# Turning one half of a token-mixing matrix before the attention inputs arrive, in an attention + mixer kernel

## The chip, the cores and the metric

The kernel runs on one core of one Trainium2 chip. The metric is device microseconds of one execution, as the median of the runs shown. A core has a matrix engine (TensorE: PE for its matmuls and PEld for its weight loads in the profile), three other compute engines (VectorE, DVE; ScalarE, ACT; GpSimd, POOL) and the sync engine (SP), each with its own in-order stream of instructions, and 16 DMA engines. Engines wait for each other through semaphores.

## The reference, cut to what matters

Attention over blocks that are mixed by a small doubly normalised matrix P comes first; its output, laid out as x with 768 tokens and 512 channels for each of 4 batches, goes through a residual mixer.

```python
P = sort_net                                   # [4, 8, 8, 8]
for _ in range(5):                             # "Sinkhorn": exp, then rows and columns normalised
    P = exp(P - max(P, -1)); P = P / sum(P, -1); P = P / sum(P, -2)
k_sorted = einsum('bhij,bhjcd->bhicd', P, k_b) # blocks of 96 keys, of 96 values, mixed by P
v_sorted = einsum('bhij,bhjcd->bhicd', P, v_b)
x = softmax(q_b @ k_sorted^T / 8) @ v_sorted   # inside each block of 96
...
a1  = alpha1 * x + beta1
tok = einsum('ts,bsd->btd', w_tok, a1)         # w_tok: 768 x 768, mixes tokens
u   = x + lam * tok
a2  = alpha2 * u + beta2
out = u + lam * (relu(a2 @ w_ch1) @ w_ch2)     # 512 -> 2048 -> 512
```

## The kernel before, in words

Batches 0 to 3 are worked through one after the other, each in two halves of 384 tokens. The channel mixer is the bulk: for every half, 16 groups of `h_ps` matmuls (`h_unit`) and 3 groups of `ch_ps` matmuls (`ch_unit`). The attention of batch b+1 is placed by hand between those groups (`put`, `run`, lines 861 to 949), so PE has channel work to do while the next batch's attention goes through the other engines. Batch 0 has no such cover: its attention is the start stage of the program, lines 794 to 852, and only its first half's channel work ends that stage.

Every engine's instructions are kept in the order in which the Python text issues them (`Engine`, lines 55 to 71). Tiles come from pools with a fixed number of buffers for each tag; a tile waits for the last use of the tile whose buffer it takes. PSUM has four small buffers (`psb`) and two of two banks (`psa`).

The start stage of batch 0, in order:

1. All large loads are DMAs that POOL issues: `q8` (two), `k8` (two), `v8` (two), the two halves of w_tok (`wt16`, two DMAs each), three broadcast vectors (`alphaB`, `betaB`, `lamB`), `W1p` and `W2p` (four each), then the raw values, keys and queries of batch 1 (`load_kv`, `load_q`). They cast from f32 to a 16-bit type. POOL's other work stands between them in the same stream.
2. The five Sinkhorn rounds (lines 302 to 319) alternate between ACT (the exponential) and DVE (sums, reciprocals, products). The table `beside` puts other work between rounds: turning the queries on PE (`q_first`), their copies out of PSUM (`q_out`), and `warm` matmuls on zeros, whose result nobody reads.
3. `mix_keys` and `mix_values` spread P into block matrices, `k_turn` and `k_copy` make the mixed, turned keys, `score` makes scores and exponentials (`et`, on ACT).
4. `v_sort` copies `v8` into `VD` with the feature index outermost, eight features a piece; `v_mix(0, n)` mixes the features 8n to 8n+7 on PE and copies them into `Vs[0]`. `pv_first(g)` needs all of `Vs[0]`; it multiplies by `et` and normalises into x on DVE, for two heads at a time.
5. The token mix of the first half of the tokens is done turned: `first_mm(g)` multiplies x by the first half of the turned w_tok (`w_tokT[:, :, 0:384]`), `first_turn(g)` turns x and adds the product of the row sums of w_tok (`rrow`) and lam·beta1 (`brow`). Out of both comes `a2T`, which the first `h_ps` matmul needs.

The turned w_tok is made in three steps for each half: `permute` copies `wt16` into `wp`, so that the 96 + 32 token rows of a panel lie side by side; `prep_wtok(ks, half)` turns panel ks in three PE transposes of 128 x 128 and copies it out of PSUM. The first half is done between the `pv_first` calls (lines 826 to 846), with row sums of w_tok by three ACT instructions (`row_sum`) that are turned in three more transposes. The second half's `prep_wtok` runs between the first `h_ps` groups.

Of the kernel before, what the change touches and what calls it, by code (L numbers as in the profile page):

```python
# [7 lines left out]
FT = mybir.dt.float32  # L8
# [8 lines left out]
def kernel(  # L17
# [25 lines left out]
    C = H * D  # L43
# [49 lines left out]
    def const(shape, dtype, name):  # L93
        return wts.tile(shape, dtype, name=name, tag=name)
# [22 lines left out]
    def load_slabs(dst, src):  # L117
        flat = src[0].rearrange("h s d -> (h s d)").rearrange("(g p f) -> p g f", p=128, f=12 * D)
        for g in range(0, H4, 2):
            pool.dma_start(dst[:, g:g + 2, :], flat[:, g:g + 2, :])  # L120

    def load_halves(dst, src):
        for th in range(2):
            pool.dma_start(
                dst[th * 64:(th + 1) * 64, :, :],
                src.rearrange("h (j th t) d -> th (h j) t d", j=NB, th=2)[th],
            )
# [12 lines left out]
    load_slabs(q8, q)  # L140
# [6 lines left out]
    dve.memset(brow[:].bitcast(FT), 0.0)  # L147
    dve.memset(rrow[:].bitcast(FT), 0.0)
# [3 lines left out]
    wt16 = []  # L152
    for half in range(2):
        t_ = att.tile([128, 3, S], F16, name="wt16", tag=("mixed", "qn")[half], bufs=1)
        for lo, n in ((0, 96), (TAIL, 32)):
            pool.dma_start(
                t_[lo // 6:lo // 6 + n],
                moe_w_tok[lo + 3 * half * n:lo + 3 * (half + 1) * n, :].rearrange("(tt p) s -> p tt s", p=n),
            )
        wt16.append(t_)  # L160
        if half == 0:
            pool.memset(VD[:, :, HB:64], 0.0)
            pool.memset(
                KT0[:].rearrange("p g i (th t) -> p (g i th) t", th=2)[:, :, HB:64].bitcast(FT), 0.0
            )

    def v_sort(lo, hi, eng):
        eng(VD[:, lo:hi, 0:HB], v8[:, :, lo:hi].rearrange("p t d -> p d t"))
# [7 lines left out]
    lamB = const([128, C], FT, "lamB")  # L176
    pool.dma_start(alphaB[:], moe_alpha1.partition_broadcast(128))
    pool.dma_start(betaB[:], moe_beta1.partition_broadcast(128))
    pool.dma_start(lamB[:], moe_lam.partition_broadcast(128))
    v_sort(16, 32, pool.tensor_copy)  # L180
    for g in range(4):
        if g == 1:
            v_sort(48, 64, pool.tensor_copy)
        pool.dma_start(W1p[:, :, g * 512:(g + 1) * 512], w1v[:, :, g * 512:(g + 1) * 512])
    pool.tensor_tensor(brow[0:1, :], bet1[:], lam1[:], ALU.mult)
# [12 lines left out]
    def load_kv(b):  # L198
        for kv, src in ((1, v), (0, k)):
            raw = att.tile([128, HB, D], F16, name="raw", tag="raw", bufs=2)  # L200
            load_halves(raw, src[b])
            raw_of[(b, kv)] = raw
# [26 lines left out]
    def warm(n, ps=psa):  # L229
        fill(ps([128, 512], FT, "warm_ps")[:], n)  # L230
# [29 lines left out]

    ab2col = const([128, 5 * CT], FT, "ab2col")

    def prep_ab2(ps):
        tps = ps([128, 4 * CT], FT, "ab2_ps")
        pe.transpose(tps[:], ab2[:], ident16f[:])
        act.copy(ab2col[:, 0:4 * CT], tps[:])
# [7 lines left out]
    rcol = const([128, 3], FT, "rcol")  # L274

    def row_sum(m):
        if m == 0:
            a1_of[0] = moep.tile([128, 8, C], F16, name="a1", tag="a1", bufs=1)
        act.activation(a1_of[0][:].rearrange("p k c -> p (k c)")[:, 0:S], wt16[0][:, m, :], AF.Copy, accum_out=rcol[:, m:m + 1])


# [5 lines left out]
    def q_first(g):  # L287
        qps[g] = q_turn(0, g, psa if g == 2 else psb)

    def q_out(g):  # L290
        for half in range(2):
            q_copy(0, g, qps[g], half, act.copy)

    beside = {
        0: [lambda: q_first(0), lambda: warm(3)],
        1: [lambda: q_first(1), lambda: warm(2), lambda: warm(3)],
        2: [lambda: q_first(2), lambda: warm(3)],
        3: [lambda: q_out(0), lambda: q_first(3)],
        4: [lambda: q_out(1), lambda: q_out(2), lambda: q_out(3), lambda: prep_ab2(psb), lambda: warm(4)],
# [20 lines left out]

    for g in range(4):
        pool.dma_start(W2p[:, g * 4:(g + 1) * 4, :], w2v[:, g * 4:(g + 1) * 4, :])
# [256 lines left out]
    w_tokT = const([128, NT, S], F16, "w_tokT")  # L579
    wp_of = {}  # L580

    def permute(half, eng, lo, hi):
        if lo == 0:
            wp_of[half] = (moep, att)[half].tile(
                [128, 3, NT, 128], F16, name="wp", tag=("u16", "raw")[half], bufs=(1, 2)[half]
            )
        wp = wp_of[half]
        src = wt16[half]
        for c0, n, w in ((0, 0, 96), (TAIL, 96, 32)):
            eng(  # L590
                wp[:, :, lo:hi, n:n + w],
                src[:, :, c0 + lo * w:c0 + hi * w].rearrange("p m (k c) -> p m k c", c=w),
            )

    def prep_wtok(ks, half, ps, eng):
        pst = ps([128, 384], F16, "wtok_ps")
        for m in range(3):
            pe.transpose(pst[:, m * 128:(m + 1) * 128], wp_of[half][:, m, ks, :], ident16[:])
        eng(w_tokT[:, ks, half * 384:(half + 1) * 384], pst[:])

    def row_sums(ps):
        rc16 = const([128, 3], F16, "rc16")
        act.copy(rc16[:], rcol[:])
        ps = ps([1, 384], F16, "rr_ps")
        for m in range(3):
            pe.transpose(ps[:, m * 128:(m + 1) * 128], rc16[:, m:m + 1], ident16[:])
        act.copy(rrow[0:1, :], ps[:])

# [17 lines left out]
    def moe_start(b):  # L626
        u_of[b] = []
        for hf in range(2):
            t_ = moep.tile([128, 3, C], FT, name=f"u32_{hf}", tag="u32", bufs=3)
            u_of[b] += [t_[:, kt, :] for kt in range(3)]  # L630
        a2T_of[b] = [moep.tile([128, CT, 384], BF, name=f"a2T_{hf}", tag="a2T", bufs=3) for hf in range(2)]
# [155 lines left out]
    def wtok(ks, eng):  # L787
        prep_wtok(ks, 0, psb, eng)

# [16 lines left out]
    v_sort(0, 8, act.copy)  # L806
    v_sort(8, 16, act.copy)
# [4 lines left out]
    v_sort(32, 48, copy)  # L812
    warm(2, psb)
    v_mix(0, 0, psb, copy)
    v_mix(0, 1, psb, copy)
    score(0, 1, 0, psa)
    v_mix(0, 2, psb, copy)
    v_mix(0, 3, psb, act.copy)
    score(0, 1, 1, psa)
    v_mix(0, 4, psb, copy)  # L820
    v_mix(0, 5, psb, copy)
    score(0, 2, 0, psa)
    v_mix(0, 6, psb, copy)
    v_mix(0, 7, psb, act.copy)
    score(0, 2, 1, psa)
    row_sum(0)
    permute(0, copy, 0, 3)
    moe_start(0)
    warm(1, psb)
    pv_first(0)  # L830
    score(0, 3, 0, psa)
    wtok(0, copy)
    wtok(1, act.copy)
    wtok(2, copy)
    permute(0, copy, 3, 6)
    row_sum(1)
    row_sum(2)
    pv_first(1)
    wtok(3, copy)
    wtok(4, copy)  # L840
    wtok(5, copy)
    permute(1, copy, 0, 6)
    score(0, 3, 1, psa)
    pv_first(2)
    row_sums(psb)
    first_mm(0, psb)
    first_turn(0, psb)
    first_mm(1, psb)
    pv_first(3)
    first_turn(1, psb)  # L850
# [3 lines left out]
    load_kv(1)  # L854
# [15 lines left out]
    for ks in range(NT):  # L870
        put(0, 0, "h", ks, lambda ks=ks: prep_wtok(ks, 1, psa, (dve.tensor_copy, act.copy)[ks % 2]))
# [108 lines left out]
```

## Time and profile before

| | |
|---|---|
| median of 3 runs | 264.29 us (263.53, 264.29, 266.08) |
| the profiled execution: its own time, its span | 263.49 us, 261.7 us |
| PE busy | 253.1 us, 97% of the span |
| DVE, ACT, POOL busy | 59%, 51%, 38% |
| granted PE clock, mean | 0.999 |
| first `h_ps` matmul | starts at 35.69 us |
| chain that ended last, by engine | PE 82%, DMA 10%, POOL 5%, DVE 2% |

The page gives busy times by engine, then by groups of instructions. In a timeline row the columns are start, length, engine, line, operation, output <- input, shape and count, and in brackets the idle time of the engine just before and what ended it; `issue` is idle time for which no semaphore accounts. Nearly all instructions carry line 65, the helper that records them, so tiles are named instead of lines.

### The profile page before, as it was taken

To read this page: it belongs to the slowest core of one execution; us is meant where nothing else is said; L and a number is where in the kernel's file an instruction comes from. 1 tells how busy PE (TensorE), PEld (TensorE's weight loads), DVE (VectorE), ACT (ScalarE), POOL (GpSimd) and SP (SyncE) were. 2 spreads that over 40 slices of the span, in tenths; PEclk is the share of its full clock that TensorE was granted. 3 is DMA by queue.
4 is the path that set the end of the run, shared out by engine and by line. 5 is a ranking of instruction groups with operands and counts; after the bars stand their busy time and mean duration, and the time that the engine had idled before them with its cause. 6 is when DMAs were issued, how large, how long until landed. Compare 5 with 4: busy or idle time off the path is not lost.

```text
span 261.7 us, 5406 instructions
## 1 busy us (share of the span) xinstructions
PE 253.1 (97%) x2179; PEld 140.2 (54%) x2179; DVE 153.8 (59%) x345; ACT 133.8 (51%) x242; POOL 100.2 (38%) x105
## 2 busy tenths in 40 slices
PE   8998799999999999999999999999999999999994
PEld 3456565555556455555565454555565445545554
DVE  6796857987658984613988643407894554051024
ACT  3568666224787539474276288573373014504700
POOL 8759304501382084612860554501302746032000
PEclk9999999999999999999999999999999999999999
DMA  6999999998979957960899859901110332112012
GB/s 101 208 206 186 206 207 213 204 147 188 159 152 183 133 125 181 130 108 3 167 178 179 121 122 170 135 20 40 46 38 0 63 93 67 23 40 80 0 43 80
DMA packets 67533, 31.04 MB, mean 119 GB/s; under 512 B 56675, under 2 KB 63219, under 8 KB 67509
## 3 DMA queue, kind: packets, MB, share of 16 engines
q0 software_dynamic: 26352, 15.34, 42.3%
q1 hardware_dynamic: 41012, 15.30, 34.3%
q8 instruction: 17, 0.28, 0.4%
q10 hardware_dynamic: 144, 0.07, 0.1%
q14 instruction: 8, 0.06, 0.1%
HBM read 32.79 MB, written 8.65 MB: 158 GB/s over the span
## 4 chain that ended last, share of the span: by engine, by line
PE 82%; DMA 10%; POOL 5%; DVE 2%; issue 1%; ACT 0%; POOLq 0%
PE ch_ps L65 32%; PE h_ps L65 30%; PE tok_ps L65 10%; DMA W2p<-in_moe_w_ch_dram 6%; DMA v<-in_v_dram 4%; PE x_ps L65 2%; PE sc_ps L65 2%; DVE a L65 2%; PE kmix_ps L65 2%; PE mix_ps L65 1%; POOL W1p L65 1%; POOL vd L65 1%; POOL k L65 1%; PE qt_ps L65 1%; POOL brow L65 0%
## 5 line engine op out<-in xcount | busy, mean ns | idle before, releaser
L65 PE MATMUL h_ps<-a2T,W1p 128*128 128x384 bf16 x512 | 91.8, 326 | 0.1
L65 ACT ACTIVATE hTa<-h_ps 128x384 bf16<-128x384 f32 x96 | 46.7, 493 | 54.0 <-PE h_ps L65 53.8
L65 PE MATMUL ch_ps<-W2p,hTa 128*128 128x512 bf16 (+2 forms) x312 | 69.0, 363 | 0.0
L65 PEld LDWEIGHTS <-W1p 128*128 128x128 bf16 x512 | 48.3, 98 | 32.3 <-issue 0.3
L65 POOL TENSOR_TENSOR ost<-ost,u 128x512 f32<-128x512 f32 x21 | 26.6, 1268 | 80.2 <-DVE ost L65 53.2
L65 DVE TENSOR_TENSOR ost<-ch_ps,lamB 128x512 f32<-128x512 f32 (+2 forms) x26 | 16.8, 648 | 54.6 <-PE ch_ps L65 54.6
L65 PEld LDWEIGHTS <-hTa 128*128 128x128 bf16 x312 | 28.7, 98 | 28.9
L65 POOL TENSOR_TENSOR u<-toktmp,x 128x512 f32<-128x512 f32 x18 | 29.6, 1650 | 32.1 <-DVE toktmp L65 32.1
L65 ACT ACTIVATE et<-sc_ps 96x768 f16<-96x768 f32 (+1 forms) x32 | 24.8, 808 | 18.9 <-PE sc_ps L65 18.9
L65 PE MATMUL tok_ps<-a,w_tokT 128*128 128x512 f16 x126 | 30.3, 379 | 0.1
L65 ACT CAST kT<-kmix_ps 64x512 f16<-64x512 f32 x32 | 22.9, 717 | 10.1 <-PE kmix_ps L65 9.8
L65 DVE TENSOR_TENSOR toktmp<-tok_ps,lamB 128x512 f32<-128x512 f32 x21 | 14.5, 690 | 20.0 <-PE tok_ps L65 18.6
L65 PE MATMUL ch_ps<-W2p,hTb 128*128 128x512 bf16 (+2 forms) x104 | 25.0, 363 | 0.0
L65 PEld LDWEIGHTS <-w_tokT 128*128 128x128 f16 x126 | 12.2, 98 | 14.0 <-DVE a L65 0.5
L65 ACT ACTIVATE hTb<-h_ps 128x384 bf16<-128x384 f32 x32 | 15.7, 490 | 7.5 <-PE h_ps L65 7.2
L65 POOL DMA_DIRECT2D qn<-in_q_dram x18 | 16.0, 910 | 6.4 <-DMA raw<-in_v_dram 6.4
L65 DVE TENSOR_TENSOR u<-toktmp,x 128x512 f16<-128x512 f32 (+1 forms) x24 | 17.0, 719 | 0.7
L65 DVE TENSOR_TENSOR x<-x_ps,rcb 96x512 f16<-96x512 f32 x24 | 16.5, 687 | 0.8
L65 PEld LDWEIGHTS <-et 96*128 96x128 f16 (+4 forms) x288 | 11.9, 100 | 5.5 <-DVE x L65 1.6
L65 PEld LDWEIGHTS <-hTb 128*128 128x128 bf16 x104 | 9.6, 98 | 9.6
L65 PE MATMUL x_ps<-Vs,et 96*128 96x65 f16 (+4 forms) x288 | 13.0, 195 | 1.7 <-DVE x L65 0.9
L65 DVE TENSOR_TENSOR a<-x,alphaB 96x512 f16<-96x512 f16 (+1 forms) x28 | 13.8, 491 | 0.0
(118 smaller groups left out, 230.1 us busy)
## 6 DMA issues: line engine op xcount, KB each, us to landing
out_dram<-ost SPq DMA_DIRECT2D x23, 192.0 KB, 2.3
raw<-in_v_dram POOLq DMA_DIRECT2D x6, 384.0 KB, 8.1
raw<-in_k_dram POOLq DMA_DIRECT2D x6, 384.0 KB, 9.9
qn<-in_q_dram POOLq DMA_DIRECT2D x18, 128.0 KB, 11.0
vscr<-mixed SPq DMA_DIRECT2D x6, 384.0 KB, 5.2
Vs<-vscr SPq DMA_DIRECT2D x3, 768.0 KB
W1p<-in_moe_w_ch_dram POOLq DMA_DIRECT2D x4, 512.0 KB, 11.5
W2p<-in_moe_w_ch_dram POOLq DMA_DIRECT2D x4, 512.0 KB, 17.3
```

What stands on the lines that cost most here:

```text
L65: ins = getattr(self.eng, name)(*args, **kwargs)
```

## The change

- `load_wtok(0)`, the first half of w_tok, becomes the first two DMAs of POOL, ahead of `q8`, `k8` and `v8`. The second half is loaded between `W1p`'s second and third quarter. `alphaB`, `betaB`, `lamB` come after the value sort, then two quarters of `W2p`; the other two come after the raw values of batch 1.
- The first half is turned straight from `wt16`, without `permute`: for each panel three pairs of transposes, one onto 96 PSUM partitions and one onto 32 (`turn_wtok`). It is done inside the Sinkhorn rounds 2 and 3; the queries move to rounds 3 and 4.
- The row sums become six PE matmuls with a column of ones against `w_tokT` (`row_sums`), in place of three ACT instructions, a cast and three transposes.
- The value sort: six of eight pieces on POOL (`n` from 2 to 7), one on DVE, one on ACT. Before, POOL and DVE had pieces of 16 features (four of eight, and two of eight), ACT two of eight.
- The second half's `permute` moves from DVE to POOL. `wp` of that half takes the buffer of tag `u16` in place of `raw`.
- Fewer and other `warm` calls; in the `v_mix` stretch, `score` calls move one place each.

```diff
+    load_wtok(0)
     ident16 = const([128, 128], F16, "ident16")
...
+    load_slabs(q8, q)
     load_slabs(k8, k)
     load_halves(v8, v[0])
     heads()
...
+    load_w1(0)
+    load_w1(1)
+    load_wtok(1)
+    load_w1(2)
+    load_w1(3)
+    for n in range(2, 8):
+        v_sort(8 * n, 8 * n + 8, pool.tensor_copy)
     pool.dma_start(alphaB[:], moe_alpha1.partition_broadcast(128))
     pool.dma_start(betaB[:], moe_beta1.partition_broadcast(128))
     pool.dma_start(lamB[:], moe_lam.partition_broadcast(128))
...
+    load_w2(0)
+    load_w2(1)
...
+    def turn_wtok(ks, ps, eng):
+        pst = ps([128, 384], F16, "wtok_ps")
+        for m in range(3):
+            c = slice(m * 128, (m + 1) * 128)
+            pe.transpose(pst[0:96, c], wt16[0][:, m, ks * 96:(ks + 1) * 96], ident16[:])
+            pe.transpose(pst[96:128, c], wt16[0][:, m, TAIL + ks * 32:TAIL + (ks + 1) * 32], ident16[:])
+        eng(w_tokT[:, ks, 0:384], pst[:])
...
+    def row_sums(ps):
+        ps = ps([1, 384], FT, "rr_ps")
+        for ks in range(NT):
+            pe.matmul(ps[:], ones16[:], w_tokT[:, ks, 0:384], start=(ks == 0), stop=(ks == NT - 1))
+        act.copy(rrow[0:1, :], ps[:])
...
     beside = {
-        0: [lambda: q_first(0), lambda: warm(3)],
-        1: [lambda: q_first(1), lambda: warm(2), lambda: warm(3)],
-        2: [lambda: q_first(2), lambda: warm(3)],
-        3: [lambda: q_out(0), lambda: q_first(3)],
-        4: [lambda: q_out(1), lambda: q_out(2), lambda: q_out(3), lambda: prep_ab2(psb), lambda: warm(4)],
+        0: [],
+        1: [],
+        2: [lambda: wtok(0, act.copy), lambda: wtok(1, act.copy), lambda: wtok(2, dve.tensor_copy)],
+        3: [lambda: wtok(3, act.copy), lambda: wtok(4, act.copy), lambda: wtok(5, dve.tensor_copy),
+            lambda: q_first(0), lambda: warm(2)],
+        4: [lambda: q_first(1), lambda: q_out(0), lambda: row_sums(psb), lambda: q_out(1), lambda: q_first(2),
+            lambda: warm(2), lambda: q_first(3), lambda: q_out(2), lambda: q_out(3), lambda: prep_ab2(psb),
+            lambda: warm(2)],
     }
...
-    v_sort(0, 8, act.copy)
-    v_sort(8, 16, act.copy)
     score(0, 0, 0, psa)
...
-    v_sort(32, 48, copy)
+    v_sort(0, 8, copy)
+    v_sort(8, 16, act.copy)
     warm(2, psb)
...
-    row_sum(0)
-    permute(0, copy, 0, 3)
+    score(0, 3, 0, psa)
+    warm(1, psb)
     moe_start(0)
-    warm(1, psb)
     pv_first(0)
-    score(0, 3, 0, psa)
-    wtok(0, copy)
-    wtok(1, act.copy)
-    wtok(2, copy)
-    permute(0, copy, 3, 6)
-    row_sum(1)
-    row_sum(2)
+    score(0, 3, 1, psa)
     pv_first(1)
-    wtok(3, copy)
-    wtok(4, copy)
-    wtok(5, copy)
-    permute(1, copy, 0, 6)
-    score(0, 3, 1, psa)
-    pv_first(2)
-    row_sums(psb)
+    permute(pool.tensor_copy)
+    load_kv(1, (1,))
+    load_w2(2)
+    load_w2(3)
     first_mm(0, psb)
     first_turn(0, psb)
+    pv_first(2)
     first_mm(1, psb)
+    first_turn(1, psb)
     pv_first(3)
-    first_turn(1, psb)
     first_mm(2, psb)
     first_turn(2, psa)
```

## The prediction

> **What bounds the kernel now.** I read the page's first and third parts, then busy time by stage, then the timelines of POOL and PE in the start stage.
>
> The page: PE is busy nearly throughout, and a small queue of its own carries instructions (packets, MB, share).
>
> ```profile
> span 261.7 us, 5406 instructions
> ...
> PE 253.1 (97%) x2179; PEld 140.2 (54%) x2179; DVE 153.8 (59%) x345; ACT 133.8 (51%) x242; POOL 100.2 (38%) x105
> ...
> q8 instruction: 17, 0.28, 0.4%
> ```
>
> Busy time of each engine in two stages (window, length, then busy us and count for PE, PEld, DVE, ACT, POOL; granted clock, DMA share, GB/s):
>
> ```profile
> 0.00:36.00 36.00, 31.57 (x583) 19.39 (x584) 27.96 (x84) 21.98 (x44) 22.48 (x36) 1.00 1.07 184
> 36.00:261.70 225.70, 221.56 (x1598) 120.85 (x1595) 125.83 (x261) 111.77 (x199) 77.75 (x69) 1.00 0.72 108
> ```
>
> From 36 us on PE is idle for 4.1 us in all, so the first h_ps matmul (35.69) sets the end: what moves it moves the end one for one. PE's work behind it is the same in both programs. So the question is when the start stage ends.
>
> POOL's timeline holds the loads (an issue, not a transfer, is the row):
>
> ```profile
> 1.25 1.57 POOL L65 DMA_DIRECT2D q<-in_q_dram  x2 [0.79 <-POOLq L964]
> ...
> 4.78 1.08 POOL L65 DMA_DIRECT2D v<-in_v_dram  x2
> ...
> 6.58 1.25 POOL L65 DMA_DIRECT2D wt<-in_moe_w_tok_dram  x2
> ...
> 12.12 0.55 POOL L65 DMA_DIRECT2D betaB<-in_moe_beta_dram  x1 [1.12 <-DMA k<-in_k_dram]
> 13.99 0.54 POOL L65 DMA_DIRECT2D lamB<-in_moe_lam_dram  x1 [1.32 <-DMA v<-in_v_dram]
> 16.57 1.51 POOL L65 COPY vd<-v 128x768 f16<-128x768 f16 x1 [2.04 <-DMA v<-in_v_dram]
> ```
>
> With issue-to-landing from each tile's answer (q 4.8 and 5.8, k's second 7.8, v's second 11.2, w_tok 12.0): q lands at 6.05 and 7.9, k by 11.9, v at 5.3 + 11.2 = 16.5, w_tok's first half at 7.3 + 12.0 = 19.3. Loads follow one another, with the DMA engines full. betaB waited for the load eight issues before it (k's second), lamB likewise (v's first): eight loads may be out.
>
> PE's timeline, around two idle times that no semaphore explains:
>
> ```profile
> 21.95 0.47 PE L65 MATMUL v_ps<-bigV,vd 64*64 64x64 f16 x19 [0.76 <-issue]
> ...
> 28.15 0.34 PE L65 MATMUL x_ps<-Vs,et 128*32 128x65 f16 x6 [0.65 <-issue]
> ...
> 35.69 0.65 PE L65 MATMUL h_ps<-a2T,W1p 128*128 128x384 bf16 x3
> ```
>
> and busy time between them:
>
> ```profile
> 21.95:28.15 6.20, 5.02 (x128) 3.85 (x128) 4.88 (x11) 5.24 (x10) 5.04 (x7) 1.00 1.17 197
> ```
>
> 128 + 128 = 256 instructions lie between the two, and 4358 PE instructions over 17 packets of q8 are 256 too: PE stops where a fetched block ends. Narrow windows of the DMA view put packets at 13.4-13.8, 19.5-19.9 and 25.6-26.0; PE passes the block edges at 16.1, 21.95 and 28.15. So a packet starts some 3.6 us after the edge before it, and its block is usable 2.3 us later: among full DMA queues PE gets 256 instructions per 5.8 to 6.2 us. This bound is in no row of waits.
>
> **The change, part by part.**
>
> *Loads.* w_tok's first half costs the stream 19.3 - 16.5 = 2.8 us and now goes first. It lands at 6.05 + 2.8 - 1.9 (a q load's spacing) = 7.0; q at 8.9 and 10.7, k by 14.7, v at 19.3. Later loads keep the sum of bytes; none runs dry: six loads (some 13 us of transfer) are out while POOL sorts. alphaB, betaB and lamB land near 34 to 36 (W1p's four quarters and w_tok's second half, at 2.5 and 2.8 us, follow v: 19.3 + 12.8 = 32.1); their first reader stood at 39.5: cover 3 us, beyond which each us costs one. W2p's last quarters and batch 1's raw loads come in another order with the same sum; raw keys lose a wait of 11.1 us on POOL that nobody waited for. Cost: none.
>
> *Turning w_tok.* Nine transposes took 0.68 us, so 0.057 each; 36 take 2.1, from 7.0 to 9.1, where PE had only zeros to multiply. Four ACT copies of 0.48: two fit into ACT's wait of 1.91 us before the fourth exponential, bar 0.2; two DVE copies of 0.35 stand in DVE's stream ahead of a round's sums, beside the exponential (0.26). P comes 0.4 late, between 0.2 and 0.9. PE itself now stands at w_tok's landing; behind it are the queries, which land at 8.9 anyway.
>
> *ACT behind the last exponential.* Six query copies took 2.31 us there; now it is eight (3.1), rrow (0.47), and a wait for the row sums (six matmuls of 384 columns, 1.15 like a tok_ps group). PE's repk stands behind the last query turn and the ab2 turn, which need buffers that those copies free: it moves from 11.88 to about 13.6. Keys come 1.7 later: third key turn 15.36 to 17.1, scores 16.46 to 18.2, DVE's last key copy to 19.3. That is when v lands, so the keys cost nothing by themselves.
>
> *The sort.* v at 19.3; POOL's piece is half of the 1.51 row, 0.76; six end at 23.9 (before: 20.6). Ahead of them POOL's sixth issue waits for k's second load (14.7), which v outlasts. The last v_mix (0.5) and its copy (0.68) let pv_first(0) start at 25.3, 1.1 late. Piece bounds: 0.62 (half of DVE's 1.23) and 1.51 (no saving from halving); I take 0.76, the same engine and access. POOL's permute (2304 elements at 1.51/768: 4.5 us) runs from about 27.3, when its half has landed, to 32; its reader stood at 38.7.
>
> [...]
>
> *What is removed between the pv_first calls*: 18 transposes, two permutes, three row-sum instructions. What is left: 1.0 for pv_first(0), 1.26 until x is normalised (25.34 to 26.60 in the trace; pv_first(1) waits for that buffer in both), then PE without waits: three each of pv_first (0.85 net of latency), first_mm (0.98), first_turn (0.33), 6.5. From 25.3 this makes h_ps start at 34.1, a gain of 1.6.
>
> *The fetch.* The changed program has the block edges at PE instructions 448, 704 and 960, counted from its start, as before. 448 is the start of the third key turn: 17.1. 704 is in v_mix(0, 3): not before 17.1 + 5.8 = 22.9. 960 is in pv_first(0), ten instructions from its end: not before 28.7 to 29.1. Before, the third edge lay inside pv_first(1), where half the chain was done; now all of it hangs on pv_first(0). From 28.7: 0.3 + 1.26 + 6.5, h_ps at 36.8 (37.2 at the upper end): 1.1 to 1.5 later than 35.69. I take 1.1. Next edge: 34.5, not late.
>
> Sum: 263.49 + 1.1 = 264.6 for a run like the profiled one, which stands 0.8 below the median of the runs (264.29); from that median 265.4. Forecast 265.0.
>
> **Rivals.**
>
> *A, faster: the fetch does not bind.* If blocks come sooner, h_ps starts at 34.1: 263.49 - 1.6 = 261.9 to 262.7 by the median. For it: the delay is seen twice. Against: DMA is as full as before in that window. Half the effect gives no change.
>
> *B, slower: POOL's sort becomes the bound.* At 1.51 a piece it ends at 28.4, pv_first(0) starts at 29.8, h_ps at 38.6, 2.9 late: 266.4 to 267.2. It decides above some 1.2 us a piece (there pv_first(0) ends after 28.7). For it: short POOL rows are dear (a 256-element copy 0.43, a DMA issue 0.55). Against: 0.43 for 256 is no more per element than 1.51 for 768; DVE's own sort copy (17.54 to 18.77) lay over POOL's, which took 1.51 with and without it.
>
> *C, slower: PE's clock drops* with the zeros gone between 6.0 and 9. The row is 1.00 in every window, with idle times up to 0.8 us among them. PE work on the key chain, some 2 us, would double: h_ps about 38.5, 266.5.
>
> [...] In the trace the clock stayed at 1.00 among transposes at 25.5 to 29, mixed with matmuls.
>
> **How the numbers follow.** Forecast case (264.0 to 266.0) 0.62; A, with its half-way forms down to 261.5, 0.20; B and C together 0.18. Range 262.6 to 267.2: it cuts off A's end and part of B and C. About 1%, 2.6 us, is what a measurement can tell from no change. Faster by that needs more than all of A: 0.05. Slower needs B or C nearly in full: 0.15. Within: 0.80.
>
> **What would show it.** Right: v lands near 19.3, six POOL pieces near 0.76, an idle time put down to issue inside pv_first(0) ending at 28 to 29, h_ps at 36.3 to 37.3. A: that idle time absent and h_ps before 35.2. B: pieces over 1.2. C: a clock under 1.00 in the first 20 us. I am wrong altogether if PE idles over 6 us after h_ps, on late W2p, raw or alphaB loads.

## The result

The changed kernel takes 275.48 us (274.96 to 275.60, 4 runs); the kernel before took 264.59 beside it (263.53 to 266.08, 4 runs). The ratio is 1.0404, with a 95% interval of 1.035 to 1.0457. The prediction, 265.0 with a range to 267.2, was wrong. The profiled execution took 274.96 us. Here and below, medians and ranges are over all runs of a kernel, and a ratio leaves out the runs that stand over 1.5% above its fastest one.

From the page of the changed kernel, the span, the busy times by engine and the granted clock in 40 slices of the span (6.83 us each, in tenths of full speed):

```profile
span 273.2 us, 5409 instructions
...
PE 261.6 (96%) x2175; PEld 145.1 (53%) x2191; DVE 152.4 (56%) x337; ACT 132.0 (48%) x237; POOL 104.1 (38%) x111
...
PEclk9659689999999999999999999999999999999999
```

The span grew by 11.5 us and PE's busy time by 8.5. (The four PE records less are gaps in the trace: the weight loads, one for each matmul, went from 2179 to 2191, so the program has 12 matmuls more.) The clock row, all nines before, has two hollows, both in the first seven slices. The view of stretches shows where the time went. First two stretches of the changed kernel, its first 36 us and all behind its first `h_ps` matmul (47.11); then the kernel before, from its first `h_ps` (35.69) on; columns as in the prediction:

```profile
0.00:36.00 36.00, 30.49 (x413) 16.66 (x415) 18.95 (x64) 14.49 (x30) 26.78 (x43) 0.77 1.06 186
...
47.11:273.20 226.09, 221.14 (x1584) 121.06 (x1597) 126.64 (x262) 112.23 (x199) 73.20 (x63) 1.00 0.65 97
```

```profile
35.69:261.70 226.01, 221.87 (x1600) 121.04 (x1597) 126.06 (x262) 112.08 (x199) 77.75 (x69) 1.00 0.73 108
```

From the first `h_ps` matmul to the end it is 226.09 against 226.01 us. The whole loss lies ahead of it: 47.11 - 35.69 = 11.42. PE's timeline there, first the rows of the kernel before to compare with:

```profile
11.88 0.25 PE L65 MATMUL repk_ps<-P,ident 32*64 32x64 f16 x4
...
24.34 1.00 PE L65 MATMUL x_ps<-Vs,et 128*128 128x65 f16 x24
...
25.55 0.68 PE L65 MATMUL wtok_ps<-ident,wp 128*128 128x128 f16 x9
```

and the changed kernel:

```profile
7.47 8.19 PE L65 MATMUL wtok_ps<-ident,wt 128*96 128x128 f16 x36 [1.32 <-DMA wt<-in_moe_w_tok_dram]
15.60 0.85 PE L65 MATMUL q_ps<-ident,q 64*64 64x64 f16 x24
...
21.98 0.25 PE L65 MATMUL repk_ps<-P,ident 32*64 32x64 f16 x4
...
30.41 0.64 PE L65 MATMUL v_ps<-bigV,vd 64*64 64x64 f16 x16 [2.37 <-DVE vd L65]
...
38.15 1.02 PE L65 MATMUL x_ps<-Vs,et 128*128 128x65 f16 x24 [0.20 <-DVE Vs L65]
...
47.11 0.65 PE L65 MATMUL h_ps<-a2T,W1p 128*128 128x384 bf16 x3
```

Three things are to be read here. The 36 transposes of w_tok hold PE for 8.19 us, where 2.1 were forecast, and `repk_ps`, which stands for "P is there and the queries are done", comes at 21.98 in place of 11.88. PE then waits 2.37 us for one DVE copy of the value sort. And the purpose of the change is met: from `pv_first(0)` (the `x_ps` row at 38.15) to `h_ps` it takes 8.96 us, against 35.69 - 24.34 = 11.35 before. So 2.4 us are gained behind `pv_first(0)`, which itself starts 13.8 late.

Two narrow stretches of the panels, PE alone (busy time and count, granted clock, DMA share, GB/s):

```profile
7.47:8.60 1.13, 1.12 (x7) 1.00 1.14 203
...
9.80:11.25 1.45, 1.45 (x7) 0.50 1.15 206
```

Each stretch holds seven transposes, one more than a panel has. From start to start in the trace, the first panel takes 1.01 us at full clock (7.48 to 8.48) and the third 1.47 at half (9.71 to 11.18). So the form of the transposes costs far more than the clock does: 0.17 us each at full clock, where the whole ones before followed each other by 0.057. The second idle time, on DVE and on POOL:

```profile
27.82 2.54 DVE L65 COPY vd<-v 128x384 f16<-128x384 f16 x1
```

```profile
27.74 2.24 POOL L65 COPY wp<-wt 128x1728 f16<-128x1728 f16 x2
```

DVE's sort copy of 384 elements takes 2.54 us (ACT's of the same shape 0.85) and lies over GpSimd's permutation, from 0.08 us behind its start to 0.38 past its end.

### The profile page after: what moved, and what is told of

Its sections match the earlier page's. It is cut to its first block, busy times and chain, and to the rows that moved or that the text cites. A ratio compares the mean times of both kernels' runs of the same rounds, so it can differ in the third digit from the quotient of the medians.

```text
span 273.2 us, 5409 instructions
## 1 busy us (share of the span) xinstructions
PE 261.6 (96%) x2175; PEld 145.1 (53%) x2191; DVE 152.4 (56%) x337; ACT 132.0 (48%) x237; POOL 104.1 (38%) x111
## 4 chain that ended last, share of the span: by engine, by line
PE 91%; DVE 4%; DMA 2%; issue 1%; ACT 0%; POOL 0%; POOLq 0%
PE ch_ps L65 30%; PE h_ps L65 30%; PE tok_ps L65 12%; PE x_ps L65 4%; PE wtok_ps L65 3%; PE sc_ps L65 3%; PE v_ps L65 2%; DMA wt<-in_moe_w_tok_dram 2%; DVE a L65 2%; PE kmix_ps L65 2%; PE mix_ps L65 1%; PE warm_ps L65 1%; PE q_ps L65 1%; DVE vd L65 1%; PE rr_ps L65 1%
## 5 line engine op out<-in xcount | busy, mean ns | idle before, releaser
L65 PE MATMUL ch_ps<-W2p,hTa 128*128 128x512 bf16 (+2 forms) x297 | 67.7, 362 | 0.8
L65 ACT CAST kT<-kmix_ps 64x512 f16<-64x512 f32 x32 | 23.0, 718 | 10.1 <-PE kmix_ps L65 9.8
L65 DVE TENSOR_SCALAR a2T<-uT,ab2col 128x384 bf16<-128x384 f16 x28 | 10.6, 441 | 6.4 <-DMA uT<-u 6.4
```

Of the source, the lines that this page charges most:

```text
L65: ins = getattr(self.eng, name)(*args, **kwargs)
```

## The experiments

First `h_ps` times are from the profiled execution, in us, so from one execution each; each ratio is against the kernel before on the same chip (263.45 to 263.95 beside the experiments). "To the end" is the span less the first `h_ps`; where it is 226.0, the start stage is the whole difference.

| run | first `h_ps` | to the end | time, us (all runs) | ratio to before, 95% |
|---|---|---|---|---|
| before | 35.69 | 226.0 | 264.59 | 1 |
| after | 47.11 | 226.1 | 275.48 | 1.035 to 1.046 |
| e1 grouped parts | 40.42 | 226.0 | 268.37 (266.5 to 271.1) | 1.009 to 1.020 |
| e2 whole panels | 37.15 | 226.0 | 266.07 (265.0 to 266.6) | 1.006 to 1.012 |
| e3 zeros first | 47.08 | 226.0 | 274.56 (274.1 to 274.9) | 1.037 to 1.044 |
| e4 permutation on DVE | 47.51 | 226.0 | 274.64 (273.3 to 275.3) | 1.036 to 1.045 |
| f1 order of the loads alone | 39.26 | 226.0 | 269.13 (267.1 to 271.4) | 1.017 to 1.030 |
| f2 matmuls as transposes | 45.62 | 226.0 | 273.92 (273.4 to 275.4) | 1.036 to 1.043 |
| f3 before, fewer zeros | 36.71 | 226.0 | 264.14 (263.1 to 267.1) | 0.999 to 1.003 |
| f4 e1, loads late | 36.67 | 239.7 | 278.13 (271.9 to 281.1) | none |
| g2 f1, zeros first | 41.01 | 226.0 | 267.40 (267.1 to 268.8) | 1.012 to 1.016 |
| g3 e1, gap in the loads | 45.45 | 226.1 | 273.51 (272.7 to 275.0) | 1.034 to 1.042 |
| g4 before, gap in the loads | 34.40 | 233.8 | 271.91 (270.0 to 275.1) | 1.023 to 1.031 |
| g5 e1 repaired | 38.11 | 239.7 | 279.45 (276.8 to 281.5) | 1.049 to 1.058 |
| h1 sort alone | 36.32 | 226.0 | 263.86 (262.4 to 264.2) | 0.997 to 1.001 |
| h2 permutation alone | 39.22 | 226.0 | 265.48 (264.2 to 267.1) | 1.004 to 1.009 |
| h3 g4, values first | 34.57 | 238.6 | 274.94 (274.5 to 275.1) | 1.040 to 1.044 |

One more arrangement, g1, has no time and no trace; h3 is nearly the same.

**The parts of a panel: e1 and e2.** e1 changes the order of the six transposes, e2 their form:

```diff
             pe.transpose(pst[0:96, c], wt16[0][:, m, ks * 96:(ks + 1) * 96], ident16[:])
+        for m in range(3):
+            c = slice(m * 128, (m + 1) * 128)
             pe.transpose(pst[96:128, c], wt16[0][:, m, TAIL + ks * 32:TAIL + (ks + 1) * 32], ident16[:])
```

```diff
-            pe.transpose(pst[0:96, c], wt16[0][:, m, ks * 96:(ks + 1) * 96], ident16[:])
-            pe.transpose(pst[96:128, c], wt16[0][:, m, TAIL + ks * 32:TAIL + (ks + 1) * 32], ident16[:])
+            pe.transpose(pst[:, c], wt16[0][:, m, ks * 128:(ks + 1) * 128], ident16[:])
```

> The changed kernel with the six transposes of a w_tok panel in another order: the three 96-column parts first, then the three 32-column parts. Nothing else. In the changed kernel's trace a panel's six take 1.13 us at granted clock 1.00 and 1.45 at 0.50, against 0.17 for three whole ones before. Theory 'change of shape': PE pays at each change between the two parts; five changes inside a panel become one, so a panel falls to some 0.5 us at full clock, the six panels end 3 to 4 us earlier, the first h_ps matmul moves from 47.1 to 43 to 44.5 and the time from 275.5 to 271.5 to 272.5. Theory 'a part is slow by itself' (each transpose 0.19 whatever stands before it): panel stays at 1.13 to 1.45 and the time within 0.7 us of 275.5. Theory 'clock alone': also no change.

> The changed kernel with each w_tok panel turned by three transposes of 128 adjacent columns in place of six of 96 and 32. The tokens then stand in another order within w_tokT's first half, so the output isn't the reference's; all other work is the same but for 18 transposes fewer. Theory 'parts': a panel takes 0.17 to 0.25 us as before the change, all six end by about 10.5 (ACT's copies then pace them), repk starts some 5 to 6 us earlier than 21.98, first h_ps near 41 to 42, time near 269.5 (the second idle time, before the values, stays or grows since v lands at 19.2 whatever happens). Theory 'clock alone': 18 transposes at half clock take 0.11 each, 2 us, and the clock still falls to 0.50 at about 9 and stays there; time near 270 to 271. The granted clock and the panel time tell these apart. Theory 'order of the loads': no gain, 275.

PE's row for the turned panels, first of e1, then of e2:

```profile
7.42 3.46 PE L65 MATMUL wtok_ps<-ident,wt 128*96 128x128 f16 x36 [1.32 <-DMA wt<-in_moe_w_tok_dram]
```

```profile
7.39 1.60 PE L65 MATMUL wtok_ps<-ident,wt 128*128 128x128 f16 x18 [1.82 <-DMA wt<-in_moe_w_tok_dram]
```

The same 36 transposes with the same operands take 3.46 us in place of 8.19 when like follows like, 0.57 a panel from start to start. So PE pays for each change between the two kinds of part, not for a part. With 6 changes for each panel in the changed kernel and 2 in e1, the difference at full clock, 1.01 - 0.57, makes 0.11 us a change (the panels of e3 at full clock, 1.04, make it 0.12). A change here is of the width, 96 or 32 columns, and of the PSUM partitions written, at once; no run separates the two.

In these two executions the clock stayed at 1.00 in e2, and in e1 up to 32.9; `repk_ps` came at 15.39 and 15.63, so of the 10.1 us that it was late in the changed kernel, 6.4 were the alternating order and the clock's fall among it. e1 comes 3.3 us behind e2 at `h_ps` for another reason, a fetch stall of 1.35 us in `pv_first(0)` with the clock halved from 32.9 to 36.3 behind it; e2 has 18 transposes and their weight loads less, so its block edges lie at other matmuls. One profiled execution is not all of them: e2's was its fastest run (264.99), and the five others, with mean granted clocks of 0.990 to 0.993, took 265.45 to 266.57; one run of e1 kept the clock at 1.00 and took 266.45.

Not every change of the width has this price. The trace of the kernel before has changes of two kinds in `pv_first(0)`: behind its one matmul of 96 columns the next one, of 128, starts 0.043 us later, but the first of 32 columns starts 0.122 us behind the last of 128, where like ones are 0.029 to 0.040 apart. Why a change costs is not shown.

**The clock: e3, f2, f3.**

e3 is the first of these edits, f2 the first and the second (the 32-column part likewise, and the PSUM tile in float32), f3 the third, on the kernel before (rounds 1 and 2 likewise):

```diff
-    warm(12)
+    warm(19)
```

```diff
-            pe.transpose(pst[0:96, c], wt16[0][:, m, ks * 96:(ks + 1) * 96], ident16[:])
+            pe.matmul(pst[0:96, c], wt16[0][:, m, ks * 96:(ks + 1) * 96], ident16[:], start=True, stop=True)
```

```diff
-        0: [lambda: q_first(0), lambda: warm(3)],
+        0: [lambda: q_first(0)],
```

> The changed kernel with 19 in place of 12 matmuls of zeros ahead of everything, which fill PE from 6.15 to about 7.6, where w_tok's first half lands; none between the panels. Theory 'the gap alone lowers the clock' (transposes count as work for the clock): granted clock 1.00 from 5.7 to the second idle time at 28, panels at 1.13 us, time 273 to 273.8. Theory 'transposes don't count': the clock falls one window later (near 12.5 in place of 9.07) and is back only at about 19 to 20; panels 1.13 for the first four, 1.45 then; time 274.3 to 275.3. Theory 'the parts, not the clock, are the cost': either way at most 2 us of the 11 come back.

> The changed kernel with 19 zeros first (so the gap before the panels is filled, as in the run with zeros first) and the 36 transposes written as ordinary matmuls against the identity into float32 PSUM: same operands, same parts of 96 and 32 columns, same order. Theory 'transposes don't count as work for the clock': the granted clock stays at 1.00 from 12.3 to 19.2, where it was 0.50 with transposes; time 273 to 273.8. Rival 'what counts is how densely PE streams, and these parts leave it idle': the clock falls near 12.3 again, time 274.3 to 275. In both a panel's six take about 1.1 us at full clock if the parts are slow for a matmul as well; if only transposes are slow, a panel falls to 0.35 and the time to 269 to 270.

> The kernel before without the 11 matmuls of zeros that stand beside its first three rounds (2.3 us of PE between 6.6 and 10.3); the 12 ahead and those behind stay. Theory 'zeros hold the clock': PE is busy some 1.7 of 3.4 us from 6 to 9, the granted clock falls to 0.50 near 9 and stays for 2 or 3 windows of 3.4 us, the key chain slows, first h_ps from 35.7 to 37 to 39, time 265 to 267. Rival 'the query turns are enough': clock 1.00 throughout, time 263.2 to 264. In the rival's case the clock of the changed kernel fell for the sake of the two-part transposes and not for want of zeros.

In e3 PE never idled ahead of the panels, and the clock fell all the same, from 12.3 to 19.2, one window later (a window: 3.41 us; the clock's changes in the changed kernel, at 9.07, 19.31, 29.55 and 36.38, lie three, three and two of them apart). `repk_ps` came 0.9 earlier, and the sort copy was done before GpSimd's permutation began, so `pv_first(0)` started at 33.66, 4.5 us earlier than in the changed kernel. Yet `h_ps` came at 47.08, because PE then stood still inside `pv_first(0)`, with the clock at half from 36.2 to 43.1:

```profile
33.66 0.52 PE L65 MATMUL x_ps<-Vs,et 128*128 128x65 f16 x11 [0.19 <-DVE Vs L65]
35.93 0.86 PE L65 MATMUL x_ps<-Vs,et 128*128 128x65 f16 x13 [1.75 <-issue]
```

In f2 the six are ordinary matmuls; PE in stretches of the clock's steps:

```profile
7.50:10.91 3.41, 3.41 (x21) 1.00 1.16 208
10.91:14.32 3.41, 3.41 (x15) 0.50 1.21 221
```

PE was busy through all of the stretch at full clock, with 21 instructions in 3.41 us, and was halved after it. So it is not that transposes don't count: matmuls in the same alternating parts lost the clock as well, and e1's 36 grouped transposes, in 3.46 us, kept it. How densely PE streams fits all three runs; no run varies that alone. In f2, too, PE stood still inside `pv_first(0)`, for 1.65 us.

f3 tests the forecast's rival C as it was put. Without the zeros the clock falls in the profiled execution (0.50 from 11.5 to 18.3) and `h_ps` comes 1.0 later. Over all runs the ratio is 1.0011 (0.9991 to 1.0032), no change that can be measured, but the ten runs are of two kinds: five kept a mean granted clock of 0.998 to 1.00 and took 263.1 to 263.8 us, five had 0.974 to 0.987 and took 264.5 to 267.1. So without the zeros the clock falls in some executions, and then it costs about 1 us and up to 3.4.

**GpSimd's permutation beside DVE: e4, h2.**

e4 edits the changed kernel, h2 the kernel before:

```diff
-    permute(pool.tensor_copy)
+    permute(copy)
```

```diff
-    permute(1, copy, 0, 6)
+    permute(1, pool.tensor_copy, 0, 6)
```

> The changed kernel with the permutation of w_tok's second half on DVE in place of GpSimd, at the same place of the program (behind pv_first(1)); nothing else. In the changed kernel DVE's one sort copy of 384 elements took 2.54 us (27.82 to 30.36) while GpSimd's permutation ran (27.74 to 29.98); PE waited 2.37 us for it, and the clock fell to 0.50 from 29.55 to 36.38. Theory 'GpSimd holds up DVE': the sort copy falls to 0.6 to 0.9 us, PE waits under 0.7 us there, the clock stays at 1.00 after 19.3, first h_ps moves from 47.1 to 42.5 to 44 and the time to 271.5 to 272.8. Rival 'that copy is slow for another reason' (DMA writes into SBUF, its access): it stays above 2 us, the clock falls as before, time 275 or later.

> The kernel before with one part of the change: the permutation of w_tok's second half on GpSimd in place of DVE, at the same place of the program; nothing else. Theory 'a DVE copy from SBUF to SBUF waits for the whole GpSimd copy': DVE's permutation of the first half (rows of 0.48 and 0.24 us at 27.05) grows to 1.5 us or more if it meets GpSimd's 2.24 us, the second three panels come 1 to 2 us later, first h_ps 36.5 to 38, time 264.8 to 266.5. Rival 'no harm': DVE is freed of 1.49 us, first h_ps 35 to 36, time 263 to 264.3. If the two do not meet in time, the rows say so and only the rival's numbers can come.

In e4 the sort copy took 0.51 us. PE's first value mix started at 28.36 in place of 30.41, but the end stayed where it was. PE's timeline of e4 shows why:

```profile
34.32 0.84 PE L65 MATMUL x_ps<-Vs,et 128*128 128x65 f16 x18 [0.19 <-DVE Vs L65]
36.66 0.35 PE L65 MATMUL x_ps<-Vs,et 128*32 128x65 f16 x6 [1.50 <-issue]
```

`pv_first(0)` now ran into a block of instructions that had not been fetched, idled 1.50 us, then 0.90 more for `et`, and the clock fell from 37.2 to 44.0. The idle time and the halved clock had only moved. DVE's sort copy of e4, for comparison with the 2.54 above:

```profile
27.80 0.51 DVE L65 COPY vd<-v 128x384 f16<-128x384 f16 x1
```

In h2, with nothing else changed, the waiting shows alone (DVE in the kernel before, then DVE, POOL and PE of h2):

```profile
27.05 0.64 DVE L65 COPY wp<-wt 128x864 f16<-128x864 f16 x2
```

```profile
26.82 2.94 DVE L65 COPY wp<-wt 128x864 f16<-128x864 f16 x2
```

```profile
27.31 2.34 POOL L65 COPY wp<-wt 128x1728 f16<-128x1728 f16 x2
```

```profile
29.82 1.14 PE L65 MATMUL wtok_ps<-ident,wp 128*128 128x128 f16 x9 [1.54 <-DVE wp L65]
```

DVE's two copies took 2.94 us in place of 0.64, PE waited 1.54, and the clock was halved from 29.0 to 35.8. This execution took 267.0, among the two dearest of ten; over all of them the permutation on GpSimd costs 0.4 to 0.9%. In e1 DVE's casts out of PSUM did not wait: five casts of the keys (18.68 to 21.35) took 2.67 us with GpSimd's sort beside them from 19.49 on, as in the changed kernel (2.67), where the sort had ended before them; DVE's sort copy, the next in e1, took 1.00 in place of the 0.51 of e4. DVE ended 0.38 and 0.11 us behind GpSimd's permutation in the changed kernel and in h2, though it started 0.08 us behind it in the first and 0.49 ahead of it in the second (26.82 against 27.31). What makes it wait is not shown.

**The order of the loads: f1, g2.** f1 is the first edit to the kernel before, g2 both:

```diff
+    load_wtok(0)
     load_slabs(q8, q)
...
+    load_wtok(1)
```

```diff
-    warm(12)
+    warm(27)
```

> The kernel before with one edit: w_tok's first half is loaded ahead of q, k and v (its second half stays where it was); it is turned, summed and used where it was before. Theory 'the order of the loads costs': v lands near 19.2 (as in the changed kernel) in place of 16.5, the sort and the values follow, first h_ps from 35.7 to 37.7 to 38.5, time from 263.5 to 265.5 to 266.3. Theory 'free' (the fetch of PE's instructions sets the pace anyway): first h_ps within 0.6 of 35.7, time 263.3 to 264.2. Theory 'it is the whole loss': time 272 or more; the run with whole panels (266.1, first h_ps 37.15) speaks against that.

> The run with the loads' order alone (269.1, between 267.05 and 271.4; granted clock 0.50 from 9.2 to 12.6) with 27 in place of 12 zeros first, so that PE is busy until the queries land at 9.4. Theory 'order plus clock': the clock stays at 1.00, the key chain is some 0.5 to 1 us shorter, first h_ps near 38.3 to 38.8, time 265.8 to 266.8, and runs lie closer together; so the order of the loads costs 2.5 us by itself and the clock the rest. Rival 'the clock is all of it': 263.5 to 264.5. Rival 'late queries alone': time stays at 267 to 271.

f1 loses about half of what the change loses (2.3% of 4.0% by the ratios; the profiled execution, 267.05, is its fastest). The queries land at 9.4 and 11.3, PE has nothing for 3.2 us, the clock is halved from 9.2 to 12.6, `repk_ps` comes at 16.52 and v lands at 19.96. With the first idle time filled but for 0.93 us (g2) `repk_ps` came at 15.61, so 3.7 us of that are the order and 0.9 the clock. With the 6.4 of e1 above, these 3.7 make up the 10.1 us by which the changed kernel's `repk_ps` was late. The time that I expected of g2 was wrong: a fetch stall of 1.31 us that ended at 25.3 halved the clock again, and `h_ps` came at 41.0. That execution was the dearest of five (268.78); three others kept a mean granted clock of 1.00 and took 267.1 to 267.4, 3.2 to 3.5 us above the kernel before, so the order of the loads costs that much without a fall of the clock. Whether a fetch stall is in it is not shown, since they have no trace. e2, whose profiled execution had neither (one idle time of 0.25 us is put to `issue`), has it together with all the rest but the parts: `pv_first(0)` 3.7 late (28.01), 2.2 gained behind it, 1.5 late at `h_ps`.

**The fetch of PE's instructions: f4, g3, g4, h3, g5.** f4 is e1 with this edit:

```diff
-    load_w1(0)
-    load_w1(1)
-    load_wtok(1)
-    load_w1(2)
-    load_w1(3)
     for n in range(2, 8):
         v_sort(8 * n, 8 * n + 8, pool.tensor_copy)
+    load_w1(0)
+    load_w1(1)
+    load_wtok(1)
+    load_w1(2)
+    load_w1(3)
```

g3 is e1 with w_tok's second half left ahead of the sort and the rest in another order behind it:

```diff
-    load_w1(0)
-    load_w1(1)
     load_wtok(1)
-    load_w1(2)
-    load_w1(3)
     for n in range(2, 8):
         v_sort(8 * n, 8 * n + 8, pool.tensor_copy)
...
-    load_w2(0)
-    load_w2(1)
+    for g in range(4):
+        load_w1(g)
...
     load_kv(1, (1,))
-    load_w2(2)
-    load_w2(3)
+    for g in range(4):
+        load_w2(g)
```

g4 does the like to the kernel before:

```diff
     for half in range(2):
+        v_sort((16, 48)[half], (32, 64)[half], pool.tensor_copy)
         t_ = att.tile([128, 3, S], F16, name="wt16", tag=("mixed", "qn")[half], bufs=1)
...
-    v_sort(16, 32, pool.tensor_copy)
     for g in range(4):
-        if g == 1:
-            v_sort(48, 64, pool.tensor_copy)
         pool.dma_start(W1p[:, :, g * 512:(g + 1) * 512], w1v[:, :, g * 512:(g + 1) * 512])
```

> The changed kernel with grouped parts (the run of 268.4 us, first h_ps 40.4) and W1p's loads and w_tok's second half issued behind GpSimd's value sort instead of ahead of it, so that the DMA engines have little to do from 19.4 to some 25. Theory 'PE's instruction fetch waits in full DMA queues': the packets that stood at 22.3 and 28.3 come within 2 us of the block edge before them (3.6 before), the idle times of 0.28 and 1.35 us put to 'issue' vanish or halve, the granted clock doesn't fall at 32.9, first h_ps 37.5 to 38.7, time 265.5 to 266.8. Rival 'a block takes some 6 us whatever DMA does': the idle times and the clock's fall stay, time 268 or more. If W1p lands too late behind its deferral, PE waits on W1p by name after 40 us and the time says nothing on the fetch; the packets still do.

> The changed kernel with grouped parts (268.4) and another order of its later loads: w_tok's second half ahead of the value sort, alphaB, betaB, lamB and W1p behind it, W2p behind batch 1's values. Theory 'fetch': no idle time over 0.4 us put to 'issue' at pv_first(0), no fall of the clock near 33, first h_ps 36.7 to 38; the loads that were too late in the run with all of them deferred are not late now; time 264.5 to 266. Rival 'later loads': PE waits behind h_ps for W1p or batch 1's values, time 267 or more though h_ps starts before 38.

> The kernel before with its loads rearranged: w_tok's first half is issued behind GpSimd's first value sort and its second half, alphaB, betaB, lamB and all of W1p behind the second; nothing else. DMA engines run dry for some 3 us when v has landed (16.5). Theory 'PE's fetch waits in full DMA queues': packets at about 16.6 and 20 to 22.5 in place of 19.7 and 25.8, the idle times of 0.76 and 0.65 put to 'issue' go, first h_ps from 35.7 to 34 to 35, time from 263.9 to 262 to 263. Rival 'the loads are the bound': what follows lands some 3.5 us later and PE waits by name for w_tok, W1p or batch 1's values; time 264 to 267.

All DMA traffic between 19.2 and 20.4 us, first in e1, then in f4, in both of which PE crossed a block's edge at about 19.1:

```profile
DMA packets 249, 0.25 MB, mean 207 GB/s; under 512 B 7, under 2 KB 249, under 8 KB 249
```

```profile
DMA packets 1, 0.02 MB, mean 14 GB/s; under 512 B 0, under 2 KB 0, under 8 KB 0
...
q8 instruction: 1, 0.02, 5.0%
```

In f4 the one packet is the instruction block, 0.30 us behind the edge; in e1 it left at 22.34, 3.2 behind it. The next one came 0.23 behind its edge, against 4.1. No idle time is put to `issue` in f4's `pv_first` calls, the clock stays at 1.00, and `h_ps` starts at 36.67 in place of 40.42. In g4 the DMA share is 0.07 or less from 16 to 19, the blocks leave at 17.55 and 23.27 (before 19.7 and 25.8), 1.0 and 2.1 us behind their edges (before 3.6 and 4.8), no idle time is put to `issue`, and the start stage gains 1.3 us: `h_ps` at 34.40. So the fetch does wait in the DMA queues, though the 1.0 us with nothing in them (1.2 in h3) shows that this is not all of its wait. But neither gain reaches the end. PE's timeline of g4:

```profile
55.61 1.01 PE L65 MATMUL mix_ps<-raw,bigM 128*128 128x512 f16 x2 [2.94 <-DMA raw<-in_v_dram]
```

What the queues did not carry while they stood empty is missing 30 us later (w_tok's first half landed at 24.0 in place of 19.3, and all loads behind it moved too): batch 1's values are late, and the clock is halved from 54.4 to 61.2. f4's runs differ by 9 us among themselves and have no ratio; only its start stage is read here. g3 missed its expectation three times: the clock's windows lay otherwise (0.50 from 7.3 to 14.2); DVE's small operations, which now met GpSimd's sort, waited piece by piece (two `ab2col` products took 1.60 us in place of 0.36); and inside `pv_first(0)` 0.99 us put to `issue` stayed, with the clock at half from 38.1 to 41.5. That block's packet left at 33.10, 3.1 us behind the edge before it, among queues that `W1p`'s loads had filled again.

h3 adds the first of these to g4; g5 is g3 with the second and third and `load_wtok(1)` behind the sort:

```diff
-    load_kv(1)
+    load_kv(1, (1,))
+    for g in range(4):
+        pool.dma_start(W2p[:, g * 4:(g + 1) * 4, :], w2v[:, g * 4:(g + 1) * 4, :])
+    load_kv(1, (0,))
```

```diff
-    warm(12)
+    warm(19)
```

```diff
-    permute(pool.tensor_copy)
+    permute(copy)
```

> The run of the kernel before with a gap in its loads (first h_ps 34.40, but PE waited 2.94 us at 52.7 for batch 1's values; time 271.9), with W2p's loads moved behind those values; nothing else. Theory 'the fetch gain can be kept': no wait over 0.5 us for batch 1's values, clock 1.00 to the end, time 262 to 263.2. Rival 'the loads are a second bound': W2p, batch 1's keys or queries come late in their place and PE waits for them by name between 55 and 75 us; time 264.5 to 272.

> The changed kernel with all the costs found so far met at once: grouped parts, 19 zeros first (no idle time ahead of the panels), w_tok's second half, alphaB, betaB, lamB and W1p issued behind the value sort (so the DMA queues are empty at two block edges), W2p behind batch 1's values, and the second half's permutation on DVE. What stays of the change: w_tok's first half is loaded ahead of q, k and v, and panels are turned in two parts. Theory 'these costs are the loss, and the order of the loads is what is left': clock 1.00 from 6 to the end of the start stage, no idle time over 0.4 us put to 'issue', first h_ps 36.3 to 37.3, time 264 to 265.5, so no gain over the kernel before. Rival 'the change is worth its purpose once repaired': first h_ps under 35, time under 263. Rival 'something not yet found': 267 or more.

With the values ahead of `W2p` (h3), the queries of batch 1 were late instead, six waits of 8.6 us in all. In g5 the start stage went as expected, clock 1.00 and no `issue` stall, and `h_ps` would have started at 36.98 but for 1.13 us on `W1p`, still 1.3 later than before the change; behind it the loads were late. Neither is a faster kernel, and no run here beat the kernel before by more than can be measured.

**The sort alone: h1**, on the kernel before:

```diff
-    v_sort(16, 32, pool.tensor_copy)
+    for n in range(2, 8):
+        v_sort(8 * n, 8 * n + 8, pool.tensor_copy)
...
-            v_sort(48, 64, pool.tensor_copy)
...
-    v_sort(32, 48, copy)
+    v_sort(0, 8, copy)
+    v_sort(8, 16, act.copy)
```

> The kernel before with one part of the change: the value sort in six GpSimd pieces of 8, one on DVE and one on ScalarE (before: GpSimd 2 pieces of 16, DVE 16, ScalarE 2 of 8). Loads, turning, permutation and row sums as before. Theory 'harmless by itself': GpSimd's sort ends at 16.6 + 4.8 = 21.4 (before 20.6), nothing waits for it by more than 0.5 us, first h_ps 35.5 to 36.3, time 263.5 to 264.6. Theory 'GpSimd and DVE hold each other up': DVE's sort copy of 384 takes 1 us or more in place of 0.5, PE waits for it, first h_ps 36.5 to 38, time 264.8 to 267, more if the clock falls.

DVE's sort copy took 1.17 us beside GpSimd's pieces, PE waited 1.03, and the time did not change: 0.9989 (0.9968 to 1.001).

## Why the prediction was wrong

- *The first `h_ps` sets the end, one for one.* Held: 226.0 to 226.1 us to the end in the eleven experiments whose later loads were in time. Held, too: the loads (w_tok's half at 7.34, forecast 7.0; v at 19.17, forecast 19.3), GpSimd's piece (0.80, forecast 0.76), and the stretch from `pv_first(0)` to `h_ps` without the removed work (8.96; 34.1 - 25.3 = 8.8 in the forecast).
- *Turning w_tok, "so 0.057 each; 36 take 2.1".* This is the step that failed. The 0.057 is the spacing of whole transposes that follow each other (the row of 0.68 holds the last one's length, too). The trace before has no row in which panels' parts alternate, and no bound was set for it. It did hold the price of a change, though: the 0.122 us between 128 and 32 columns in `pv_first(0)`, 0.09 more than between like ones. An estimate from that, 36 changes beside the 2.1, would have been 5.3 us. Measured: 0.17 each at full clock, 8.19 us for the 36 with the clock's fall. e1 showed that the change of shape is what costs.
- *"P comes 0.4 late, between 0.2 and 0.9."* It followed from that step. The panels' copies stand in ACT's and DVE's streams ahead of the next round's exponential and sums, and ACT waited 6.4 us for PE there, DVE 5.8. The last product of P moved from 11.51 to 17.20. The forecast counted the copies' own 0.48 and 0.35 us, and not the wait for PE ahead of each.
- *ACT behind the last exponential, `repk_ps` 1.7 late (13.6).* Too short by 1.8 even where the panels are whole: 15.39 in e2, where PE waited for the queries until 10.12 (forecast 8.9) and the last P came at 12.86. g2 has the order of the loads without the added work on ACT, and its `repk_ps` came at 15.61. So the lateness goes with the queries' landing and with what PE's own stream holds behind them (in e2 no idle time from 11.63 to 15.39), and not with ACT's copies, where the forecast looked for it.
- *The sort, "pv_first(0) start at 25.3, 1.1 late".* Two slips of the sum that the forecast does not hang on: 23.9 + 0.5 + 0.68 is 25.1, and 25.3 is 1.0 behind 24.34. In e2 it started at 28.01.
- *Rival C, the clock.* It came, but its place and price were wrong. It was priced at 2.8 us once, for the key chain, and for want of the zeros; with the zeros gone and nothing else (f3) it came in half of the executions and cost about 1 us and up to 3.4 there. In the changed kernel it fell twice, for 10.2 and 6.8 us, once among alternating parts and once behind an idle time.
- *"POOL's permute ... its reader stood at 38.7", cost nothing.* Its length was over-estimated (4.5, measured 2.24), but the cost was looked for at its reader only. It lay in the DVE copy beside it: 2.37 us of PE and the second fall of the clock.
- *The fetch, "I take 1.1".* Right as a mechanism (f4, g4), and seen where the forecast put it, inside `pv_first(0)`, in e1 (1.35 us), e3 (1.75), e4 (1.50), f2 (1.65) and g3 (0.99). In the changed kernel PE was too late to meet it. It was mis-sized in one way: behind such a stall the clock was halved for 3.4 us (e1, g3) or 6.8 (e3, e4), which the forecast left out.

With whole panels, time and first `h_ps` are near those of the forecast (266.07 for the median, 37.15 in the fastest run; forecast 265.0 and 36.8), but that is luck and not its terms: `pv_first(0)` starts 2.7 later than forecast and meets no stall.

## What to carry to other kernels

Cost a matmul or transpose from a row in which the one before it has the same shape, and look at the order: shapes that alternate cost 0.11 to 0.12 us at each change here, and grouping like with like gave back 6.7 of the 11.4 us here without any other edit. When work is put between the steps of a chain that two engines carry, price the wait of those engines for it, not only its own length (6.4 us on ACT and 5.8 on DVE here). A copy moved to GpSimd is not free even when its reader is far away: list the DVE copies from SBUF to SBUF that will run beside it (2.54 us in place of 0.51 and 2.94 in place of 0.64 here).

## What the runs showed of the hardware

- A change between transposes of 96 and of 32 columns cost 0.11 to 0.12 us at full clock (e1 against the changed kernel and e3), and matmuls in the same order were no faster (1.04 us a panel in f2 and in e3). Between 128 and 96 columns no such cost shows (0.043 us from start to start, against 0.122 from 128 to 32, `pv_first(0)` before).
- The clock fell after a window of 3.41 us in which PE was busy throughout, but with 21 sparse instructions (f2); it came back after one (f1) to four windows (g5, behind late loads).
- The packet of a block of 256 PE instructions left 0.2 to 1.2 us behind the edge before it with empty DMA queues (f4, g4, h3), and 2.1 to 4.8 with full ones (g4, e1, before).
- Idle times moved rather than vanished: taking one of 2.4 us away (e4, e3) let PE meet a fetch stall of 1.5 or 1.75 and lose the clock there.
